# Separate PSUM tiles for the transposed q and k of the first two head pairs

## The chip, the cores and the metric

The kernel runs on one core of a Trainium2 chip. The metric is the device time of one execution in microseconds. Three runs of the kernel before gave 801.07, 801.15 and 801.8 us; their median, 801.15 us, is the time before.

The core's engines work side by side, each through its own list of instructions in order, and they wait for each other through semaphores: PE (TensorE, matrix products; PEld is its loading of weights), DVE (VectorE), ACT (ScalarE), POOL (GpSimd) and SP (SyncE, which here issues nearly all DMAs).

## The reference

Attention with normalised queries and keys, followed by a feed-forward block. Cut to what is computed:

```python
# q, k, v: (8, 12, 448, 64)
q_n = q / sqrt(mean(q*q, -1) + 1e-6) * g_q          # the same for k with g_k
scores = q_n @ k_n.T / sqrt(64)
attn = softmax(scores)
x = (attn @ v)  ->  (8*448, 12*64)
h = x @ w_in                                         # (3584, 768) @ (768, 1024)
solu = h * softmax(h)
y = (solu - mean) / sqrt(var + 1e-6) * g_ln @ w_out  # (3584, 1024) @ (1024, 768)
```

All values are float32.

## The kernel before

The kernel holds two versions of the whole computation. The one that runs with these inputs is `fast_path`; a flag computed from the data sends the work to the other one only when the data leave a range. All that follows is `fast_path`.

Attention works on pairs of heads, 48 in all, and two pairs make a quad `m` of 24. For every pair there is a tile `qkT` with the two heads' dimensions on 128 partitions and the 448 positions of q, then of k, along the row. `scores(n, kc)` (L819) multiplies 128 of k's positions with all of q's, for both heads, into one PSUM tile `s` of two banks; `scores_last` (L832) does the remaining 64 positions for both pairs of a quad at once, so it needs the `qkT` of both. ACT takes the exponential of each such tile (L809) into an SBUF tile `E`. DVE and POOL add up exponentials (`es`, L846 and L858), PE multiplies them with v (L869, L883, L910) and sums the denominators (`sm`, L932), and DVE divides (L958).

Pairs from the third on are loaded and normalised in a blocked layout and transposed by DVE: squares on ACT (L672), row sums on DVE (L680), a fold of these sums over partitions on POOL (L690 four copies, L691 an addition), a reciprocal root (ACT L697 and L698, DVE L704 to L707), the multiplication on POOL (L713), the transposition on DVE (L723), and a factor on q's half on ACT (L727).

The first two pairs, n = 0 and n = 1, go another way, to have something to multiply early. `load_rows` brings their rows in, `square_rows` (L748, L750), `sum_rows` (L756) and the same reciprocal root give the norms, `normalise_rows` (L775, DVE, first q then k) writes the normalised rows over the squares, `transpose_rows` (L783) transposes them on PE by four products with an identity matrix for q (s = 0) and four for k (s = 1) into PSUM, and `take_rows` copies them from PSUM to `qkT`: q on ACT with its factor (L791), k on ACT for pair 0 (L793) and on DVE for pair 1 (L795).

[...] Tag "t" has three buffers of two banks each, which are taken in turn: by the gain column `pg` (L491), by the score tiles `s`, and by `sm`. Tag "o" has one buffer of two banks: it serves the five products of `warm_up` (L766) ahead of the work, then the transposed rows `pt` of pairs 0 and 1, one tile for q and k together (q in the first bank, k in the second), and then the attention output `o` of each quad.

The order of the instructions on every engine is the order in which the program writes them (`manual_schedule`). Semaphore waits are put in by the tile framework: an instruction waits for what it reads, and for the last readers and writers of what it overwrites. The built kernel's waits show that this goes by whole tiles: PE's transpositions of k wait for ACT though ACT only reads q's bank of that tile, and L791 waits for k's transpositions where these precede it. A new tile in a used buffer waits for the last users of that buffer.

In the program the start reads as follows: for pair 0, both halves are transposed, then both are taken (L791, L793). Then come the scores of pair 0 (`scores(a, 0)` to `scores(a, 2)`), and between them and `scores_last` stands pair 1:

```python
                unit(lambda: scores(a, 2))
                squares_half(3, 0, True)
                for s in range(2):
                    transpose_rows(1, s)
                    take_rows(1, s)
                squares(2)
                squares_half(3, 1, False)
                add(a)
                add_more(a)
                row_sums(2)
                unit(lambda: scores_last(m))
```

So on ACT the three exponentials of pair 0 stand ahead of L791 of pair 1, and `squares(2)` and half of `squares(3)` behind it, before the exponential of `scores_last`; on PE the transpositions of q and of k stand ahead of `scores_last`.

Of the kernel before, what the change touches and what calls it, by code (L numbers as in the profile page):

```python
# [9 lines left out]
FP32 = mybir.dt.float32  # L10
# [356 lines left out]
def fast_path(  # L367
# [25 lines left out]
    B, H, S, D = q.shape  # L393
    DM, DFF = moe_w_in.shape
    P = 128
# [25 lines left out]
    ps_t = banks_in.enter_context(tc.tile_pool(name="ps_t", bufs=3, space=bass.MemoryType.PSUM))  # L421
# [346 lines left out]
    def flat(x):  # L768
        return x.rearrange("p h j d -> p (h j d)")
# [6 lines left out]

    def transpose_rows(n, s):
        d = st[n]
        if s == 0:
            d["pt"] = ps_t.tile([P, 2, 512], FP32, tag="o", name="pt", bufs=1)  # L780
        d["pt", s] = d["pt"][:, s, 0:S]
        for j in range(4):
            nc.tensor.transpose(  # L783
                d["pt", s].rearrange("p (r j) -> p j r", j=4)[:, j], flat(d["sq"][:, s])[:, j * P : (j + 1) * P], ident[0:R, 0:R]
            )
# [627 lines left out]
    with tc.manual_schedule():  # L1413
# [10 lines left out]
        for s in range(2):  # L1424
            normalise_rows(0, s)
            transpose_rows(0, s)
# [6 lines left out]
        for m in range(NQ):  # L1433
# [21 lines left out]
            if m == 0:  # L1455
# [6 lines left out]
# [3 lines that stand above are left out]
# [289 lines left out]
```

## Time and profile before

| | us |
|---|---|
| median of three runs | 801.15 |
| profiled execution | 802.04 |
| its span | 800.2 |
| PE busy | 786.5 (98%) |
| DVE busy | 609.2 |
| POOL busy | 524.3 |
| ACT busy | 473.3 |
| PE busy, 0 to 10.77 | 8.01 |
| PE busy, 10.77 to 16.35 | 4.44 |
| PE busy, 16.35 to 30.25 | 12.89 |
| PE busy, 30.25 to the end (770.0) | 761.12 |

The span is the time from the first to the last instruction of the profiled execution; what lies around it makes the difference to that execution's time. The clock granted to PE was 0.999 over the span. The four stretches at the end of the table cut the start of the kernel at points where PE waited. Busy time is an average over stages with different limits, so for a change in one place the timeline of that place and the chain of waits say more. A row of the timeline gives start and duration in us, engine, line, operation, what is written and read, and how many instructions it merges; the bracket tells how long the engine had been idle before, and what ended that.

### The profile page before, as it was taken

The page shows a single profiled execution, that of the slowest core. Times are in us where ns is not written, and L with a number is a line of the kernel's source. Part 1 is how long each engine was busy: PE and PEld are TensorE (multiplying, and loading weights), DVE is VectorE, ACT ScalarE, POOL GpSimd, SP SyncE. Part 2 cuts the span into 40 slices and gives each one's busy share as a digit, 9 for nine tenths or more (in the row PEclk, how much of TensorE's full clock was granted, in tenths as well). Part 3 has the DMA queues.
Part 4 walks back from the last instruction along what each step waited for, and adds up shares of the span by engine and source line. Part 5 has one row for each costly group of instructions (what it writes and reads, how often), then busy time and mean ns, then how long its engine had stood idle before and what let it go on. Part 6 is the DMA issues. An engine that isn't in the chain of part 4 may idle for free.

```text
span 800.2 us, 15287 instructions
## 1 busy us (share of the span) xinstructions
PE 786.5 (98%) x5382; PEld 469.2 (59%) x5382; DVE 609.2 (76%) x1153; ACT 473.3 (59%) x783; POOL 524.3 (66%) x665
## 2 busy tenths in 40 slices
PE   8999999999999999999999999999999999999997
PEld 3344444444444444444444444444789999999996
DVE  6777989889888895487777667776896776866945
ACT  6777888878778773566766544454515455464410
POOL 2666677768877785243466466668597777877861
PEclk9999999999999999999999999999999999999999
DMA  8878798998888742455555445542757557466212
GB/s 165 162 163 166 171 187 195 197 188 170 166 162 176 147 117 71 138 132 151 151 132 143 108 106 145 140 122 52 208 149 234 166 174 255 133 212 236 100 60 84
DMA packets 266913, 122.74 MB, mean 153 GB/s; under 512 B 184012, under 2 KB 251980, under 8 KB 266828
## 3 DMA queue, kind: packets, MB, share of 16 engines
q1 hardware_dynamic: 252988, 111.78, 55.9%
q10 hardware_dynamic: 13840, 9.90, 4.5%
q8 instruction: 44, 0.72, 0.4%
q14 instruction: 41, 0.34, 0.1%
HBM read 84.94 MB, written 36.70 MB: 152 GB/s over the span
## 4 chain that ended last, share of the span: by engine, by line
PE 88%; DVE 4%; POOL 2%; SPq 1%; ACT 1%; DMA 1%; issue 1%; DVEq 0%; ACTq 0%; POOLq 0%
PE A L1253 14%; PE s L819 13%; PE o L883 12%; PE BD L1038 12%; PE A L1038 12%; PE B L1253 7%; PE sm L932 5%; PE C L1038 5%; PE C L1253 3%; PE s L832 2%; PE o L869 2%; SPq L636 1%; PE o L910 1%; DMA ur<-ud 0%; DVE ub L1142 0%
## 5 line engine op out<-in xcount | busy, mean ns | idle before, releaser
L809 ACT ACTIVATE E<-s 128x896 f32<-128x896 f32 x168 | 141.4, 933 | 12.8 <-PE s L819 11.6
L819 PE MATMUL s<-qkT 64*64 64x448 f32 x1152 | 124.0, 544 | 1.6 <-ACT qkT L793 1.2
L883 PE MATMUL o<-E,v 64*64 64x448 f32 x1056 | 107.2, 536 | 0.0
L1127 POOL TENSOR_TENSOR he<-he,mhalf 128x1 f32<-128x1 f32 x28 | 27.3, 975 | 104.2 <-DVE he L1126 99.1
L819 PEld LDWEIGHTS s<-qkT 64*64 64x64 f32 x1152 | 49.8, 163 | 58.2 <-issue 25.2
L858 POOL TENSOR_TENSOR es<-es,E 128x896 f32<-128x896 f32 x23 | 49.1, 2135 | 51.4 <-DVE es L846 51.4
L1253 PE MATMUL A<-w_out,sums 128*128 128x192 f32 x392 | 80.1, 327 | 2.2 <-POOL sums L1233 1.3
L1253 PE MATMUL B<-w_out,sums 128*128 128x192 f32 x392 | 79.9, 326 | 0.4 <-DVE P L1315 0.4
L713 POOL TENSOR_TENSOR qkn<-qk,ny 128x896 f32<-128x896 f32 x46 | 77.1, 1697 | 3.5 <-DVE ny L707 1.5
L1038 PE MATMUL A<-w_in,xg 128*128 128x512 f32 x168 | 74.6, 593 | 0.0
L883 PEld LDWEIGHTS o<-E,v 64*64 64x64 f32 x1056 | 40.6, 133 | 58.0 <-issue 58.0
L1109 ACT ACTIVATE u<-h,hmax 128x1024 f32<-128x1024 f32 x28 | 32.2, 1151 | 66.8 <-DVE hmax L1103 66.8
L1038 PE MATMUL BD<-w_in,xsum 128*128 128x512 f32 x156 | 71.2, 592 | 0.0
L1253 PEld LDWEIGHTS A<-w_out,sums 128*128 128x128 f32 x392 | 66.1, 190 | 3.3 <-POOL sums L1233 1.6
L1253 PEld LDWEIGHTS B<-w_out,sums 128*128 128x128 f32 x392 | 66.3, 190 | 0.8 <-DVE P L1315 0.7
L846 DVE TENSOR_TENSOR es<-E 128x896 f32<-128x896 f32 x48 | 56.9, 1189 | 0.7 <-ACT E L809 0.7
L1038 PEld LDWEIGHTS A<-w_in,xg 128*128 128x128 f32 x168 | 31.8, 190 | 40.1 <-issue 39.3
L723 DVE STREAM_TRANSPOSE qkT<-qkn 128x896 f32<-128x896 f32 x46 | 50.9, 1106 | 4.1 <-POOL qkn L713 4.1
L1038 PEld LDWEIGHTS BD<-w_in,xsum 128*128 128x128 f32 x156 | 29.5, 190 | 37.5 <-issue 35.2
L690 POOL COPY ss<-part 32x56 f32<-32x56 f32 x92 | 47.1, 512 | 6.1 <-DVE part L680 1.9
L680 DVE TENSOR_REDUCE part<-sq 128x28 f32<-128x896 f32 x46 | 47.8, 1077 | 2.2 <-ACT sq L672 2.2
L1253 PE MATMUL A<-w_out,s 128*128 128x192 f32 x224 | 45.7, 326 | 0.0
(160 smaller groups left out, 1665.5 us busy)
## 6 DMA issues: line engine op xcount, KB each, us to landing
ur<-ud SPq DMA_DIRECT2D x60, 256.0 KB, 4.4
ud<-ub SPq DMA_DIRECT2D x112, 128.0 KB, 2.3
xd<-xo SPq DMA_DIRECT2D x48, 224.0 KB, 3.0
qk<-in_q_dram SPq DMA_DIRECT2D x92, 112.0 KB, 3.2
qk<-in_k_dram SPq DMA_DIRECT2D x92, 112.0 KB, 3.1
v<-in_v_dram SPq DMA_DIRECT2D x24, 384.0 KB, 5.2
out_dram<-P SPq DMA_DIRECT2D x19, 384.0 KB, 3.4
raw<-in_moe_w_in_dram SPq DMA_DIRECT2D x12, 512.0 KB, 5.1
```

The costliest lines, as they stand in the source:

```text
L680: nc.vector.tensor_reduce(norms[m]["part"][:, i], st[n]["sq"], AX, OP.add)
L690: e.tensor_copy(ss[g * 32 : g * 32 + 32], part[o * 32 : o * 32 + 32])
L713: e.tensor_tensor(d["qkn"].rearrange("p (s b) d -> p s b d", s=2), d["qk"].rearrange("p s (b d) -> p s b d", d=32), y.rearrange("p (s b) - ...
L723: nc.vector.transpose(d["qkT"].rearrange("p s t -> p (s t)"), d["qkn"].rearrange("p b d -> p (b d)"))
L809: nc.scalar.activation(d["E", kc], s[:, :, 0:S], AF.Exp)
L819: nc.tensor.matmul(s[c : c + D, h, 0:S], d["qkT"][hh, 1, keys], d["qkT"][hh, 0, :], start=True, stop=True,)
L846: nc.vector.tensor_tensor(d["es"], d["E", 0], d["E", 1], OP.add)
L858: e.tensor_tensor(d["es"], d["es"], d["E", 2], OP.add)
L883: x = nc.tensor.matmul(d["o"][h * D : (h + 1) * D, :], quads[m]["v"][pp, i + 2 * h, kc], d["E", kc][pp, h], start=False, stop=(part == 1 a ...
L932: nc.tensor.matmul(sm[g : g + 32, :], ones[:, w], e[:, h, t * S // 2 : (t + 1) * S // 2], start=(x == 0), stop=(x == len(terms) - 1),)
L1038: nc.tensor.matmul(k[bank], a[:, c], w_in[i][:, c], start=begin and c == 0, stop=c == HD - 1, skip_group_check=not begin,)
L1253: nc.tensor.matmul(k[bank], a[:, c].rearrange("p a i -> p (a i)"), w_out[:, area, i, c], start=begin and c == 0, stop=c == KC - 1, skip_gr ...
```

## The change

`transpose_rows` no longer takes one tile for q and k of a pair. It takes a tile of two banks for each and uses the first bank of it. The tile has tag "o" only for q of pair 1; the other three (q and k of pair 0, k of pair 1) have tag "t", with its three buffers.

```diff
     def transpose_rows(n, s):
         d = st[n]
-        if s == 0:
-            d["pt"] = ps_t.tile([P, 2, 512], FP32, tag="o", name="pt", bufs=1)
-        d["pt", s] = d["pt"][:, s, 0:S]
+        pt = ps_t.tile([P, 2, 512], FP32, tag="o" if n and s == 0 else "t", name="pt", bufs=1 if n and s == 0 else 3)
+        d["pt", s] = pt[:, 0, 0:S]
         for j in range(4):
             nc.tensor.transpose(
                 d["pt", s].rearrange("p (r j) -> p j r", j=4)[:, j], flat(d["sq"][:, s])[:, j * P : (j + 1) * P], ident[0:R, 0:R]
             )
```

In the built kernel the instructions of each engine and their order are the same as before; the waits of ten or so instructions in the start-up differ. On PE, pair 0's q transpositions and pair 1's no longer wait for PE's own earlier work, the second and third scores of pair 0 do, and the first and third product of `scores_last` (L832) have a wait for ACT in place of one for PE and beside one for DVE. On ACT, L793 has a wait for PE of its own. On DVE, L795 loses its wait for ACT, and L846 behind it gets one. Line numbers behind `transpose_rows` are smaller by one in the changed kernel.

## Prediction

> **What bounds the kernel now.** First the page's chain of work that ended last, by engine:
>
> ```profile
> PE 88%; DVE 4%; POOL 2%; SPq 1%; ACT 1%; DMA 1%; issue 1%; DVEq 0%; ACTq 0%; POOLq 0%
> ```
>
> Then PE's own waits over the first 100 us (us in total, times, longest):
>
> ```profile
> PE s L819 <- ACT qkT L793: 1.2, 1, 1.2
> PE pt L783 <- ACT qkT L791: 1.1, 1, 1.1
> PE s L832 <- ACT E L809: 0.7, 1, 0.7
> ```
>
> PE is the bound (786.5 us busy of 800.2), but not from the start. Between 100 and 400 us PE has no wait at all in that view; the last long idle of the start-up ends at 30.25 us. What the change touches lies in the start-up, 8 to 16 us, so I read the engines' timelines there (start, duration; merged rows; in brackets the idle time before and its releaser).
>
> ```profile
> 8.87 0.61 ACT L748 ACTIVATE xsq<-x 112x512 f32<-112x512 f32 x1
> 9.66 0.64 ACT L791 ACTIVATE qkT<-pt,gcol 128x448 f32<-128x448 f32 x1 [0.17 <-PE pt L783]
> 10.19 0.53 ACT L793 COPY qkT<-pt 128x448 f32<-128x448 f32 x1
> ...
> 11.85 2.54 ACT L809 ACTIVATE E<-s 128x896 f32<-128x896 f32 x3 [0.68 <-PE s L819]
> 14.26 0.65 ACT L791 ACTIVATE qkT<-pt,gcol 128x448 f32<-128x448 f32 x1
> 14.78 0.97 ACT L672 ACTIVATE sq<-qk 128x896 f32<-128x896 f32 x1
> 15.62 0.60 ACT L667 ACTIVATE sq<-qk 128x448 f32<-128x448 f32 x1
> 17.37 2.54 ACT L809 ACTIVATE E<-s 128x896 f32<-128x896 f32 x3 [1.16 <-PE s L832]
> ```
>
> ```profile
> 13.22 0.60 PE L783 MATMUL pt<-ident,xsq 112*128 112x112 f32 x4
> 14.96 0.60 PE L783 MATMUL pt<-ident,xsq 112*128 112x112 f32 x4 [1.14 <-ACT qkT L791]
> ...
> 15.67 0.62 DVE L795 COPY qkT<-pt 128x448 f32<-128x448 f32 x1 [2.00 <-PE pt L783]
> 16.21 1.08 DVE L846 TENSOR_TENSOR es<-E 128x896 f32<-128x896 f32 x1
> ```
>
> See the detour: pair 1's k transpositions (14.96) wait for ScalarE's reading of q (14.26 to 14.91), though q lies in the other bank. ScalarE came to that late, being in its three exponentials; then DVE's copy, the second half of the L832 scores (16.35) and ScalarE's next exponential (17.37) each wait in turn. The chain view walks through just these: ACT L791, PE L783, DVE L795, DVE L846, then POOL L858 (17.44), POOL L690 (19.61), POOL L691 (21.48), ACT L697 (21.82), and on to PE L832 at 30.25. A microsecond saved here therefore moves the point from which PE runs dense.
>
> **The change part by part.** No instruction is added or removed except waits, and every engine's order is the same. Three more tiles are drawn from tag "t" (three buffers), a full turn, so everything after them gets the buffer it had.
>
> *Pair 0's q reading (L791 at 9.66).* With one tile it waits for both transpositions (they end at 8.38+1.18 = 9.56); with its own it waits for q's, which end at 8.96. ScalarE is then free: L748 ends at 8.87+0.61 = 9.48, and consecutive ScalarE rows overlap by 0.10 (L793 starts at 10.19, L791 ends at 10.30). New start 9.39, gain 0.27. L793 now waits for k's transpositions itself (9.56), in time for its 9.92. The 0.27 carries: scores at 10.50 instead of 10.77, first exponential at 11.58, L697 at 10.34 instead of 10.61 (its sums are ready at 10.28), so DVE's normalising and PE's q transpositions of pair 1 move too, 13.22 to 12.95.
>
> *Pair 1's k transpositions (L783 at 14.96).* The wait for L791 goes. In its place comes a wait for the reader of the buffer that they now take: by the count of the turns (gain column, q, k, scores 0, 1, 2) the first scores' buffer, so the first exponential, over at 11.85+0.92-0.27 = 12.50. k's normalised rows are there at 12.86 (DVE row 11.84+1.29, less 0.27). So they follow q's directly: the four q rows start 0.1 apart, k's first goes in at 13.30, the last ends 0.62 later, at 13.93. Behind this wait stand the L832 scores and all of PE; cover is 13.30-12.50 = 0.8 us, and each us of exponential beyond that would cost one.
>
> *Waits of scores.* The second and third scores wait for q's and k's transpositions (over by 9.56, needed at 10.96): nothing. L832 waits for the second exponential instead of the first (13.3, PE comes at 13.83): nothing. The later scores' first tiles, L819 at 16.36 and after, have buffers whose readers (third exponential, DVE copy) end before the L832 scores that precede them: nothing.
>
> *What follows.* DVE's copy starts at 13.97 instead of 15.67 (DVE is free at 13.40), its sum L846 at 14.51 instead of 16.21. ScalarE: L791 at 13.99, L672 at 14.51, L667 at 15.35 to 15.95. L832's second half needs the copy (over at 14.60) and L791 (14.64): 14.69 instead of 16.35; the exponential follows 1.02 later, as before (16.35 to 17.37): 15.71. But ScalarE is in L667 until 15.95, less the overlap 0.10: about 15.84. Gain on ScalarE 17.37-15.84 = **1.53**. Of this 0.27 is the first step, 1.16 the idle time in the row, 0.10 the overlap.
>
> *POOL.* Its sum L858 follows DVE's: 17.44 becomes 15.74. The row-sum copies follow it:
>
> ```profile
> 17.44 2.11 POOL L858 TENSOR_TENSOR es<-es,E 128x896 f32<-128x896 f32 x1 [10.88 <-DVE es L846]
> 19.61 1.79 POOL L690 COPY ss<-part 32x56 f32<-32x56 f32 x4
> 21.48 0.30 POOL L691 TENSOR_TENSOR ss<-ss,part 128x56 f32<-128x56 f32 x1
> ```
>
> Four copies of 0.22 us should take about 1.0, not 1.79: in the chain the third has 1.00 us (20.14 to 21.14), as long as DVE's second sum L846 (19.94 to 21.04) runs. That sum waits for an exponential and gains 1.53, to 18.41; the copies gain 1.70, to 17.91, 18.17, 18.43. So it is a tie whether the third copy gets in ahead. [...] By the row the second copy (19.87 to 20.09) was running when the sum began and the sum still took 1.10 against 1.08 of its sister, so a copy may slip in free: L691 at 19.69, a gain of 1.79. I take 1.53, with 1.79 as the near end of the range: times 799.6 and 799.4.
>
> *From there to 30.25.* L697, the second pair's normalising, the transposes and the next exponential release one another. PE's share: the L819 scores that wait for the exponential (18.34) move to 16.81, the dense stretch to 26.6 ends at 25.1, next scores 25.45 instead of 26.98. Loads do not move, since SP issues without pause until 33.5: the squares at 23.15 move to 21.62, and their last load is issued by 18.03, landing in 3.1 (page) at 21.1 at the latest. The values' v was issued at 10.01 and takes 5.2; it is needed at 20.26-1.53 = 18.7. Nothing else before 36 us is fresh.
>
> *After 30.25.* PE is busy 761.1 of the 770.0 us to the end, at a granted clock of 1.00, and its idle there (1.3 and 0.6 us the longest waits) ends on POOL, ScalarE or DVE, which move along. Loads after 40 us wait on SP for PE and DVE, so they move too. Gain at the end 1.53.
>
> **Sum.** On the profiled execution: span 800.24-1.53 = 798.7; with the 1.8 around it (802.04-800.24), 800.5. The median of the runs is 0.89 below that execution: 801.15-1.53 = **799.6**.
>
> **Rivals.**
>
> *The new wait takes part of it.* PE's wait names ScalarE, not which exponential. Were it the third (ends 14.39-0.27 = 14.12), k's transpositions would go at 14.16, the copy at 14.83, L832's second half at 15.50, the exponential at 16.52: gain 0.85, 800.3. The count of turns speaks against it. Likewise DVE's copy now reads PSUM beside ScalarE, which it didn't before: doubled to 1.24 it would end at 15.21 and leave 1.1, 800.1.
>
> *Nothing comes through.* The start-up could hang on loads, with the queue busy until 33.5 whatever PE does (DMA share 0.97 from 16.35 to 30.25). If the squares still began at 23.15, all would be as before: 801.1. For this a load would have to land 2 us later than computed; no wait of ScalarE for a load shows in the start-up after 5 us.
>
> *Slower.* One place can turn it: between the two feed-forward products PE waits on data written to DRAM and read back; the chain has 3.68 us for ur<-ud at 565.55, and PE's idle there is 0.57 and 1.31. If, arriving 1.53 earlier, these reads met other traffic and took over 5.2 us, the gain would be gone; the page's median is 4.4, and later ones reach 7. At 7.0: 801.15-1.53+3.3 = 802.9. Against it: that other traffic is issued behind the same compute and moves along.
>
> **How the numbers follow.** Likeliest 0.72: 799.6, own range 799.2 to 800.0. Partly taken 0.12: 800.1 to 800.6. Nothing 0.10: 801.1. Slower 0.06: 802.9. The range 799.2 to 801.1 leaves out the slower case, the upper part of the third, and a little of the first below. The measurement of this kernel can tell about 0.2% (1.6 us) from no change, so the border is 799.55, just under my value: of the likeliest 0.72, the branch of 1.79 (0.3) is past it, and a third of the rest (0.14). Faster 0.44, same 0.50, slower 0.06.
>
> **What would show it.** After: k's second transpositions start at 13.3 with no wait for L791; ScalarE's 1.16 us of idle before the fourth exponential gone, that row at about 15.8; L791 first at 9.4; POOL L691 at 19.7 to 20.0; PE's last start-up wait over at 28.7 instead of 30.25; from there equal lengths. It would be wrong if the fourth exponential came before 16 but PE's dense stretch still began at 30, or if that began at 28.7 and the end did not move.

## The result and the profile after

The changed kernel takes 799.89 us in the median of 18 runs (799.25 to 800.51); the kernel before, run beside it, 801.52 (801.07 to 802.3). The ratio is 0.9978, with a 95% interval of 0.9971 to 0.9984: 1.6 us less, or 0.22%, in an interval of 0.16% to 0.29%. The profiled execution has 800.01 us and a span of 798.2.

The changed kernel's timeline of ScalarE (start and duration in us; the bracket is the idle time before and what ended it):

```profile
7.46 1.15 ACT L748 ACTIVATE xsq<-x 112x512 f32<-112x512 f32 x2
8.95 0.64 ACT L790 ACTIVATE qkT<-pt,gcol 128x448 f32<-128x448 f32 x1 [0.34 <-PE pt L782]
9.55 0.53 ACT L792 COPY qkT<-pt 128x448 f32<-128x448 f32 x1
...
11.22 2.54 ACT L808 ACTIVATE E<-s 128x896 f32<-128x896 f32 x3 [0.65 <-PE s L818]
13.62 0.65 ACT L790 ACTIVATE qkT<-pt,gcol 128x448 f32<-128x448 f32 x1
14.14 0.97 ACT L672 ACTIVATE sq<-qk 128x896 f32<-128x896 f32 x1
14.98 0.59 ACT L667 ACTIVATE sq<-qk 128x448 f32<-128x448 f32 x1
15.45 2.55 ACT L808 ACTIVATE E<-s 128x896 f32<-128x896 f32 x3
```

The 1.16 us of idle time ahead of the fourth exponential are gone; it starts at 15.45 instead of 17.37. ScalarE works without a break from the first exponential to the end of the sixth (18.00). Its first reading of q starts at 8.95 instead of 9.66; it now follows the end of q's transpositions (8.85) and no longer that of k's (9.52).

PE and DVE of the same kernel, their timelines:

```profile
12.59 0.98 PE L782 MATMUL pt<-ident,xsq 112*128 112x112 f32 x8
13.50 1.47 PE L831 MATMUL s<-qkT 64*64 64x448 f32 x6
...
13.61 0.62 DVE L794 COPY qkT<-pt 128x448 f32<-128x448 f32 x1 [0.55 <-PE pt L782]
14.15 1.08 DVE L845 TENSOR_TENSOR es<-E 128x896 f32<-128x896 f32 x1
...
18.03 1.09 DVE L845 TENSOR_TENSOR es<-E 128x896 f32<-128x896 f32 x1 [0.81 <-ACT E L808]
```

All eight transpositions of pair 1 are now one group of 0.98 us: k's follow q's without a wait. DVE's copy of k no longer stands behind ScalarE's reading of q (13.61 and 13.62, side by side).

POOL:

```profile
15.38 2.10 POOL L857 TENSOR_TENSOR es<-es,E 128x896 f32<-128x896 f32 x1 [8.86 <-DVE es L845]
17.54 1.93 POOL L690 COPY ss<-part 32x56 f32<-32x56 f32 x4
19.56 0.30 POOL L691 TENSOR_TENSOR ss<-ss,part 128x56 f32<-128x56 f32 x1
```

And PE's waits over the first 100 us (in total, times, longest):

```profile
PE pt L766 <- DVE warm L763: 1.4, 1, 1.4
PE pt L782 <- DVE xsq L775: 0.9, 1, 0.9
PE s L831 <- ACT E L808: 0.7, 1, 0.7
PE s L818 <- ACT qkT L792: 0.6, 1, 0.6
PE s L818 <- ACT qkT L727: 0.4, 1, 0.4
```

The wait of 1.1 us on L791 is missing. The last start-up wait, ahead of L831, has kept its 0.7 us and is over at 28.31 instead of 30.25.

To see where the 1.94 us at that point come from, the start-up is cut at four instructions that every kernel has: PE's first transposition, the first exponential, the fourth, and PE's first product with v of the second quad (L869 before, 34.06 us). The last column runs from there to the end of PE's last product.

| | first transposition | to first exponential | to fourth | to second quad | to PE's end |
|---|---|---|---|---|---|
| before | 8.38 | 3.47 | 5.52 | 16.69 | 760.60 |
| after | 8.25 | 2.97 | 4.23 | 16.67 | 760.45 |
| difference | 0.13 | 0.50 | 1.29 | 0.02 | 0.15 |

Pair 1's tiles bring 1.29 us, pair 0's 0.50 in this execution. The 0.13 of the first column is not the change's: that column goes with the loads and with the end of the warm-up products, and lies between 8.09 and 8.51 in the other profiles that ran five of them, with and without the change. The 0.15 of the last column lies in one wait of PE near 568 us, 0.57 us before and 0.41 after; its cause stays open.

### The profile page after: what moved, and what is told of

It reads as the page before. It is cut to its first block, busy times and chain, and to the rows that moved or that the text cites. A ratio compares the mean times of both kernels' runs of the same rounds, so it can differ in the third digit from the quotient of the medians.

```text
span 798.2 us, 15285 instructions
## 1 busy us (share of the span) xinstructions
PE 785.4 (98%) x5382; PEld 469.1 (59%) x5382; DVE 608.6 (76%) x1153; ACT 472.2 (59%) x783; POOL 523.8 (66%) x665
## 4 chain that ended last, share of the span: by engine, by line
PE 87%; DVE 5%; SPq 2%; DMA 2%; ACT 1%; POOL 1%; issue 1%; DVEq 0%; ACTq 0%; POOLq 0%
PE A L1252 14%; PE s L818 13%; PE o L882 12%; PE BD L1037 11%; PE A L1037 11%; PE B L1252 7%; PE sm L931 5%; PE C L1037 5%; PE C L1252 3%; PE s L831 2%; PE o L868 2%; SPq L636 1%; DVE ub L1141 1%; PE o L909 1%; DMA ur<-ud 1%
## 5 line engine op out<-in xcount | busy, mean ns | idle before, releaser
L690 POOL COPY ss<-part 32x56 f32<-32x56 f32 x92 | 47.2, 513 | 6.1 <-DVE part L680 1.9
```

What stands on the lines that cost most here:

```text
L690: e.tensor_copy(ss[g * 32 : g * 32 + 32], part[o * 32 : o * 32 + 32])
```

## Experiments

All runs stand beside runs of the kernel before on the same chip. Their start-ups, cut in the same way from each profile (the warm-up's duration is the PE L766 row, discussed further down):

| | warm-up | first transposition | to first exp. | to fourth | to second quad | to PE's end | median us | ratio, 95% interval |
|---|---|---|---|---|---|---|---|---|
| pair 1 split | 6.76 | 8.36 | 3.56 | 4.23 | 16.68 | 760.47 | 799.87 | 0.9979 (0.9971 to 0.9988) |
| pair 0 split | 6.10 | 8.09 | 2.97 | 5.51 | 16.66 | 759.79 | 800.92 | 0.9988 (0.9979 to 0.9997) |
| other order | 6.56 | 8.10 | 3.47 | 4.78 | 16.67 | 759.64 | 800.71 | 0.9993 (0.9983 to 1.0003) |
| sum inside | 6.92 | 8.36 | 3.40 | 4.23 | 16.09 | 759.63 | 799.32 | 0.9972 (0.9962 to 0.9982) |
| sum behind | 7.06 | 8.51 | 3.40 | 4.23 | 16.46 | 759.85 | 799.44 | 0.9972 (0.9962 to 0.9983) |
| gain later | 6.30 | 8.24 | 2.97 | 4.23 | 16.67 | 760.44 | 799.75 | 0.9977 (0.9967 to 0.9987) |
| both | 5.54 | 8.17 | 2.97 | 4.23 | 16.09 | 759.66 | 798.63 | 0.9965 (0.9951 to 0.9979) |
| before, gain later | 6.32 | 8.23 | 3.47 | 5.51 | 16.66 | 760.60 | 801.18 | 0.9995 (0.9986 to 1.0004) |
| after, six products | 6.72 | 8.22 | 3.35 | 4.23 | 16.66 | 760.44 | 800.15 (one run) | |
| gain later, six products | 7.52 | 8.96 | 2.90 | 4.23 | 16.68 | 759.68 | 799.67 (one run) | |

The columns to the fourth exponential and to the second quad repeat to 0.03 us wherever a kernel has the same part. The column to the first exponential does not: it has 2.90 to 3.40 where pair 0 has its own tiles and 3.47 to 3.56 where it shares one, which is taken up below. Times alone would not tell parts of 0.3 us apart.

**One pair alone.** Both kernels draw three tiles of tag "t", so that the later turn of the buffers is as in the others.

```diff
 # pair 1 split: pair 0 shares one tile
-        if s == 0:
-            d["pt"] = ps_t.tile([P, 2, 512], FP32, tag="o", name="pt", bufs=1)
-        d["pt", s] = d["pt"][:, s, 0:S]
+        if s == 0 or n == 1:
+            d["pt"] = ps_t.tile([P, 2, 512], FP32, tag="t", name="pt")
+        d["pt", s] = d["pt"][:, s, 0:S] if n == 0 else d["pt"][:, 0, 0:S]
 # pair 0 split: pair 1 shares one tile
+        if s == 0 or n == 0:
+            d["pt"] = ps_t.tile([P, 2, 512], FP32, tag="t", name="pt")
+        d["pt", s] = d["pt"][:, s, 0:S] if n == 1 else d["pt"][:, 0, 0:S]
```

> Only pair 1's q and k have tiles of their own; pair 0 still shares one tile. All three tiles have tag t, so the turn of the buffers ends as in both kernels. Theory (pair 1's k transpositions waiting for ScalarE's reading of q is the larger part of the gain): k transpositions follow q's at about 13.6 us, DVE's copy at about 14.3 instead of 15.67, the fourth exponential at about 16.1 instead of 17.37, so 1.25 us less than before, 0.35 to 0.6 us more than the changed kernel. Rival (the early q reading of pair 0 brings most): 0.5 us less than before or nothing.

> Only pair 0's q and k have tiles of their own; pair 1 shares one. Theory: k transpositions of pair 1 still wait for ScalarE's q reading, ScalarE's idle time of about 1.16 us before the fourth exponential stays, and everything from the first scores on comes 0.3 us earlier when the warm-up products run late and 0.6 us earlier when they run early: 0.3 to 0.6 us less than before. Rival (it doesn't carry, since pair 1 waits for its own sums): nothing.

With pair 1 split, ScalarE's timeline has no gap ahead of the fourth exponential:

```profile
11.92 2.54 ACT L809 ACTIVATE E<-s 128x896 f32<-128x896 f32 x3 [0.68 <-PE s L819]
...
15.68 0.59 ACT L667 ACTIVATE sq<-qk 128x448 f32<-128x448 f32 x1
16.15 2.55 ACT L809 ACTIVATE E<-s 128x896 f32<-128x896 f32 x3
```

With pair 0 split the gap is there, and the q reading is early:

```profile
8.78 0.63 ACT L791 ACTIVATE qkT<-pt,gcol 128x448 f32<-128x448 f32 x1
...
16.57 1.73 ACT L809 ACTIVATE E<-s 128x896 f32<-128x896 f32 x2 [1.16 <-PE s L832]
```

The two parts are independent in these profiles: 5.52 to 4.23 by pair 1's tiles alone (1.29), 3.47 to 2.97 by pair 0's alone (0.50). Pair 1's part is the larger; the rival that gave it to pair 0 is out. In times, pair 1 split alone is not told apart from the changed kernel, though 0.35 to 0.6 us were expected between them.

**The wait has two places.** The shared tiles stay, but pair 1's transpositions both precede the readings.

```diff
                 for s in range(2):
                     transpose_rows(1, s)
+                for s in range(2):
                     take_rows(1, s)
```

> The shared tiles of before; in the program pair 1's two transpositions stand ahead of the two readings. PE no longer waits for ScalarE's q reading, but DVE's copy of k does, because the two read one tile. Theory (tracking by whole tiles, in two places): k transpositions at about 13.8, DVE's copy right behind the q reading at about 14.95 instead of 15.67, the fourth exponential 0.7 us earlier: 0.7 us less than before, about half of what the separate tiles give. Rival (the wait on PE alone is the cost): as much as pair 1's own tiles, 1.25 us less.

All engines' timeline of this run:

```profile
12.93 0.99 PE L783 MATMUL pt<-ident,xsq 112*128 112x112 f32 x8
...
13.97 0.65 ACT L791 ACTIVATE qkT<-pt,gcol 128x448 f32<-128x448 f32 x1
...
14.66 0.62 DVE L795 COPY qkT<-pt 128x448 f32<-128x448 f32 x1 [1.28 <-ACT qkT L791]
```

PE is free of the wait, and DVE has it: it stands idle for 1.28 us ahead of its copy of k. The last 0.7 of these pass between the end of k's transpositions (13.92) and the end of ScalarE's reading of q (14.62) from the same tile's other bank. The fourth exponential gains 0.74 (5.52 to 4.78), where separate tiles give 1.29. So a bit over half of pair 1's part could be had by order alone, and the rest is the wait between the two readers of one tile. In times this run is not clear of no change.

**The long copy of POOL.** In the changed kernel the third of the four copies L690 has 1.14 us where the others have 0.22. Two kernels move DVE's second sum of exponentials out of its way.

```diff
 # sum inside: add(b) between the first and the second step of the root
-    def rsqrt_step(d):
+    def rsqrt_step(d, between=None):
         nc.vector.tensor_scalar(x, ss, -0.5 / D, -0.5e-6, OP.mult, OP.add)
+        if between:
+            between()
...
-                rsqrt_step(norms[m + 1])
+                rsqrt_step(norms[m + 1], (lambda: add(b)) if m == 0 else None)
...
-                add(b)
                 norms_next()
 # sum behind: add(b) behind all of norms_next()
-                add(b)
                 norms_next()
+                add(b)
```

> The changed kernel with DVE's second sum of exponentials (pair 1) moved behind the first of DVE's four steps of the reciprocal root, that is behind POOL's fold of the row sums. Theory (POOL's third copy takes 1.0 us only because that sum runs): all four copies 0.22 us, POOL's addition at about 18.7 instead of 19.56, the start-up over 0.75 us earlier: 0.75 us less than the changed kernel (0.4 to 0.9), 2.4 us less than before. Rival (the long copy has another cause, or the loads set the time by now): no less than the changed kernel.

> The changed kernel with DVE's second sum of exponentials moved behind all four steps of the reciprocal root, that is to the same moment as POOL's normalising (L713). Theory (the two engines exclude each other while both read two SBUF inputs): POOL's fold is fast as in the run with the sum inside, but POOL's first normalising then waits for the sum or the sum for it, and about 0.6 us or all of the gain over the changed kernel is lost: 799.9, within 0.4 us of the changed kernel. Rival (only the small copies collide, the normalising does not): as fast as the run with the sum inside, 0.6 us less than the changed kernel.

POOL with the sum inside:

```profile
18.09 1.01 POOL L690 COPY ss<-part 32x56 f32<-32x56 f32 x4
19.18 0.30 POOL L691 TENSOR_TENSOR ss<-ss,part 128x56 f32<-128x56 f32 x1
```

POOL and DVE with the sum behind:

```profile
18.24 1.02 POOL L690 COPY ss<-part 32x56 f32<-32x56 f32 x4
...
21.14 4.14 POOL L713 TENSOR_TENSOR qkn<-qk,ny 128x896 f32<-128x896 f32 x2 [1.49 <-DVE ny L707]
...
20.98 1.08 DVE L845 TENSOR_TENSOR es<-E 128x896 f32<-128x896 f32 x1
```

In both the four copies take 1.0 us, not 1.93: the sum was the cause. With the sum behind, POOL's normalising begins 0.16 us after the sum's start and takes 4.14 us for the two instead of 3.36: the collision has moved there. That a sum of DVE holds up POOL is thus seen at two places, with a small and a large POOL instruction; the small copy was held to the sum's end, the large one by 0.78 of the 0.92 us that the sum still ran. The copy L690 reads one tile, and its third one took 1.14 us in the changed kernel beside the sum where the others took 0.22; so the theory's condition, two inputs on both sides, is not what the runs show. Of the gain the sum inside keeps 0.58 us (16.67 to 16.09), less than the 0.75 expected: POOL's addition comes 0.92 us earlier, counted from the first exponential, but then DVE's other three steps of the root wait for the sum of 1.09. The sum behind keeps 0.21, where nothing or little was expected. The medians do not tell these two kernels from each other or from the changed one (ratios 0.9972, 0.9972 and 0.9978).

**The squares behind the warm-up.** Pair 0's part is 0.50 us in one profile and nearly nothing in another (3.40 against 3.47 with the sum inside and behind). ScalarE's copy of the gain column (L492) waits for PE behind the warm-up products, and pair 1's squares (L748) stand behind that copy. PE's and ScalarE's rows of the kernel before:

```profile
1.37 6.72 PE L766 MATMUL pt<-warm 128*128 128x448 f32 x10 [1.37 <-DVE warm L763]
...
8.27 0.16 ACT L492 COPY gcol<-pg 128x1 f32<-128x1 f32 x1 [1.48 <-PE pg L491]
```

Of the changed kernel:

```profile
1.37 5.84 PE L766 MATMUL pt<-warm 128*128 128x448 f32 x10 [1.37 <-DVE warm L763]
...
7.39 0.16 ACT L492 COPY gcol<-pg 128x1 f32<-128x1 f32 x1 [0.65 <-PE pg L491]
```

Of the run with the sum inside:

```profile
1.37 6.92 PE L768 MATMUL pt<-warm 128*128 128x448 f32 x10 [1.37 <-DVE warm L765]
...
8.54 1.15 ACT L750 ACTIVATE xsq<-x 112x512 f32<-112x512 f32 x2
9.59 0.61 ACT L792 ACTIVATE qkT<-pt,gcol 128x448 f32<-128x448 f32 x1
```

The same ten records take from 5.54 to 7.06 us in the profiles, since they start 0.75 us apart at first and 0.38 later, and the point of that step differs. When the warm-up is long, as with the sum inside, the squares last until 9.69 and the q reading comes at 9.59, later than the end of k's transpositions (9.44). Five kernels test it: the gain column's copy moved behind the squares, on the changed kernel, on the one with the sum inside, and on the one before; and six warm-up products instead of five, with and without this move.

```diff
+    def gain_turned():
         pg = ps_t.tile([P, KF], FP32, tag="t", name="pg")[:, 0:1]
         nc.tensor.transpose(pg, gg[:, 2:4].rearrange("o h d -> o (h d)"), ident[0:1, 0:1])
         nc.scalar.copy(gcol[:, KF : KF + 1], pg)
...
         for s in range(2):
             square_rows(1, s, nc.scalar)
+        gain_turned()
...
 # six products
-        for _ in range(5):
+        for _ in range(6):
```

> The changed kernel; ScalarE's small copy of the gain column, which waits for PE behind the warm-up products, moves behind pair 1's squares, so that these no longer wait for the warm-up. Theory (pair 0's own tiles bring 0.5 us when the warm-up ends early and nearly nothing when it ends late, because ScalarE's squares stand in the way then): the q reading starts within 0.1 us of the end of q's transpositions [...]; 0 to 0.5 us less than the changed kernel, about 0.2 in the median. Rival: no difference.

> The sum inside and the gain column later, both on the changed kernel. If both theories hold the gains add: about 0.8 us less than the changed kernel, 2.4 to 2.6 us less than before. If loads set the start-up by now, not below the run with the sum inside.

> The kernel before with the gain column later. Theory: nothing is gained, because ScalarE's q reading of pair 0 waits for k's transpositions anyway, which end at about 9.56: no more than 0.1 us less than before. Rival (the squares held by the warm-up cost time by themselves): 0.2 us or more less than before.

> The changed kernel with six warm-up products instead of five. Theory: ScalarE's squares of pair 1 wait, behind the gain column, for the end of the warm-up, 0.75 us later than with five, and hold up the q reading of pair 0: it starts 0.4 us or more after the end of q's transpositions, against 0.1 in the changed kernel's profile, and the first exponential comes about 3.4 us after the first transposition instead of 2.97. Rival (the warm-up has nothing to do with it): 2.97 us as before.

> The same six products, with the gain column's copy behind the squares. Theory: the squares no longer wait for the warm-up; the q reading starts within 0.1 us of the end of q's transpositions or of the gain column's copy, and the first exponential comes 2.97 us after the first transposition, as long as the warm-up ends before PE's first transposition is ready. Rival: as with the squares behind the gain column, about 3.4 us.

ScalarE with six products on the changed kernel:

```profile
8.27 0.16 ACT L492 COPY gcol<-pg 128x1 f32<-128x1 f32 x1 [1.56 <-PE pg L491]
8.34 1.15 ACT L748 ACTIVATE xsq<-x 112x512 f32<-112x512 f32 x2
9.39 0.61 ACT L790 ACTIVATE qkT<-pt,gcol 128x448 f32<-128x448 f32 x1
```

With the gain column later as well:

```profile
6.66 1.13 ACT L750 ACTIVATE xsq<-x 112x512 f32<-112x512 f32 x2
9.07 0.16 ACT L494 COPY gcol<-pg 128x1 f32<-128x1 f32 x1 [1.28 <-PE pg L493]
9.67 0.63 ACT L792 ACTIVATE qkT<-pt,gcol 128x448 f32<-128x448 f32 x1 [0.43 <-PE pt L784]
```

With the squares held back by the sixth product, pair 0's part falls from 0.50 to 0.12 (2.97 to 3.35), although the step in the warm-up came early in that execution. With the squares freed it is back (2.90), although there the warm-up itself ran past the first transposition's data and PE was late (8.96), so that the first exponential came at 11.86, later than the 11.57 with the squares held back: the two single executions show the interval and no gain in time. On the kernel before the move does nothing (3.47, ratio not clear of 1): its q reading waits for k's transpositions anyhow. On the changed kernel alone the profile fell in an execution with a short warm-up, where nothing was to be gained, and the median shows no gain that could be told from none; the 0.2 us expected are neither shown nor excluded. These two kernels make the cleanest pair for the change itself: the squares are out of the way in both, the warm-ups are alike (6.32 and 6.30 us), the first transpositions too (8.23 and 8.24), and separate tiles save 0.50 to the first exponential and 1.28 from there to the fourth.

**The version with both** takes 798.63 us beside 801.31 before, a ratio of 0.9965 (0.9951 to 0.9979) and 2.68 us less, where 2.4 to 2.6 were expected; it beats both kernels in the medians, though its interval still overlaps that of the changed kernel. Its second quad starts at 31.46, against 32.12 in the changed kernel and 34.06 before. Of these 0.66 us the sum brings 0.58 and the earlier first transposition 0.08; the gain column's move brought nothing in this execution, whose warm-up was the shortest of all, so that the profile doesn't show the two gains adding up.

## Why the prediction was right

- *The sum.* Forecast 799.6 us, a gain of 1.53, with 799.2 to 801.1 as the range; measured 799.89, a gain of 1.63 on runs side by side. On the profiled span 798.7 was forecast and 798.2 measured, a gain of 2.03 instead of 1.53, and two of the signs listed came 0.4 us earlier than forecast (fourth exponential 15.45 for 15.84, last start-up wait over at 28.31 for 28.7). That the gain of the medians comes within 0.1 us of the forecast is in part luck, since one of its terms was mis-sized in both directions (pair 0's, below). The median before, 801.52, lies besides in a gap: nine of its 18 runs have 801.07 to 801.34 and nine 801.70 to 802.3, which fits the two groups of the last section. The means of the 18 runs differ by 1.69 us.
- *Pair 1's transpositions and DVE's copy.* Forecast for the way from the first to the fourth exponential: 1.16 of idle time and 0.10 of overlap, 1.26. Measured 1.29, in every kernel with pair 1 split.
- *Pair 0's q reading* is the term that was mis-sized: 0.27 forecast, 0.50 measured in the profile and 0.07 in two others (with the sum inside and behind). The step took ScalarE's squares at 8.34 to 9.48 as fixed, from one profile; they move with the warm-up's end. With 1.29 the two ends make 1.36 and 1.79, and the median of 1.63 lies between.
- *The new waits cost nothing*, as forecast: k's transpositions follow q's with no gap, though they wait for the first exponential's buffer. The rival that PE would wait for the third exponential (0.85 gained) is out: k's started at 13.03, the first exponential had ended at 12.13, and the third ended at 13.75. The rival that DVE's copy would slow down beside ScalarE's reading of PSUM is out too: 0.62 us as before.
- *POOL's tie.* The third copy began 0.04 us after DVE's sum and was held until 19.21, 0.09 after the sum's end; the addition L691 gained 1.92, just what the fourth exponential gained (17.37 to 15.45). The branch in which the third copy slips ahead did not happen in any profile that had the collision: the sum began first in all, and that copy took 1.00 to 1.15 us. That POOL would gain 1.53 here and not 1.79 was the author's estimate, and no run shows either: the runs show L691 gaining what the sum ahead of it gained, 1.92 beside 1.91 (19.94 to 18.03). Where the second copy was first, its row in the prediction is borne out: in four profiles (before, pair 0 split, other order, before with the gain column later) the second copy had about 0.15 us to run when the sum began, and the sum took 1.09 to 1.10 us; it has 1.09 where no copy was running, and held to the copy's end it would have had 1.24. With larger POOL instructions both orders show a wait, 0.27 to 0.55 us on DVE and 0.33 to 0.46 on POOL (last section).
- *The carry.* From the fourth exponential to the second quad 16.69 and 16.67, from there to PE's end 760.60 and 760.45: what the start-up saves arrives whole. Neither the loads (nothing comes through) nor the DRAM round trip at 565 us (slower) took any of it in these two profiles. The chain of the changed kernel does lead through a load of v, which lands at 21.21, just ahead of ScalarE's L672 at 21.22. But L672 starts 0.80 us after the start of the exponential ahead of it in all twelve profiles, the kernel before included, so ScalarE's own order sets it and not that load. The loads did not stand still as forecast: the one of v that was issued at 18.92 before was issued at 18.02; it was issued at 17.44 in the kernel before with only the gain column moved, so this differs from execution to execution.
- *The chances.* The gain of 0.22% lies just beyond the border of 0.2%, but its interval of 0.16% to 0.29% holds the border, and 799.89 is above the 799.55 that the forecast named for it. The runs do not decide between "faster" (0.44) and "same" (0.50).

## What to carry to other kernels

Where waits are tracked by whole tiles, two independent streams that share one tile wait for each other though they touch different banks, and the wait shows twice: for the writer behind the first reader (1.14 us of PE in the kernel before) and between the two readers (0.7 us of DVE with the other order). Order alone removed one of the two here; separate tiles removed both, and cost nothing: the buffer that k of pair 1 takes had been read 0.9 us before it was needed. Ahead of a dense stretch of 760 us the saving of the start-up arrived one for one, but its size must be read from several profiles when something in it, here the warm-up, ends at another time in every execution.

## What was not expected

- The step in the pace of the warm-up products (0.75 to 0.38 us from start to start) came anywhere from about 4.5 to 7.5 us in the twelve profiles (worked out from the starts of the records): these start 0.75 us apart up to 6.75 us in the kernel before and up to 4.52 in the changed kernel, and 0.38 apart from 7.17 and 5.17. The profile's row of granted clock shows 9 tenths and more throughout, so it doesn't tell of this step; the spacing of the PE L766 records does. The trace's first record of the granted clock, which is 1.0, begins within the step in both, at 6.82 and 5.06 us; ahead of it there is none. No run here shows what sets that moment; the spread is 3 us. Where pair 0 has its own tiles and the squares stand behind the gain column, the first exponential came 2.97 us after the first transposition with warm-ups of 5.84 and 6.10 us, 3.35 with one of 6.72, and 3.40 with those of 6.92 and 7.06; where pair 0 shares a tile it came after 3.47 to 3.56 with any warm-up.
- From the second quad to PE's end the profiles fall into two groups, 759.6 to 759.9 and 760.4 to 760.6, whichever kernel it is. They part between 575 and 585 us, where PE waits about 0.8 us in one group and 1.3 in the other (or 0.3 and 1.05 in two waits). The view of waits puts this down to POOL's sums, but PE starts 0.15 us after the end of DVE's `u<-A,P` in all twelve profiles. The traces show what delays that: again an addition of DVE beside one of POOL. First the changed kernel with the gain column later, of the longer group, then the version with both, of the shorter:

```profile
577.64 0.73 POOL L1233 TENSOR_TENSOR sums<-sums,a 128x256 f32<-128x256 f32 x1
577.73 1.19 DVE L1221 TENSOR_TENSOR s<-a,s 128x512 f32<-128x512 f32 x1
...
579.11 0.34 DVE L1268 TENSOR_TENSOR u<-A,P 128x192 f32<-128x192 f32 x1
```

```profile
576.83 0.65 DVE L1223 TENSOR_TENSOR s<-a,s 128x512 f32<-128x512 f32 x1
577.01 1.06 POOL L1235 TENSOR_TENSOR sums<-sums,a 128x256 f32<-128x256 f32 x1
...
577.67 0.34 DVE L1270 TENSOR_TENSOR u<-A,P 128x192 f32<-128x192 f32 x1
```

In all six profiles of the longer group POOL's addition begins first, and DVE's then takes 0.92 to 1.20 us; in all six of the shorter DVE's begins first and takes 0.65, and POOL's takes 1.06 to 1.19 instead of 0.73. So here each engine holds up the other, whichever comes second. The order goes with the landing of a read from DRAM (`ur<-ud`): ScalarE's copy that waits for it starts 543.03 us or more after the second quad in the longer group and 542.97 or less in the shorter. This is read from the traces alone; no run here forces the order.
